# The last loads, the last sums and the last store of a decode kernel: w4 in other pieces, the result on 8 neighbouring partitions, wq in one load

## The chip, the cores and the metric

One core of a Trainium2 chip. The metric is the device time of one execution in microseconds; the tables give medians of several executions. A profile is one execution on the same core; its span is about 1.7 us shorter than the time of that execution (211.0 us of span belong to 212.7 us of time). PE is TensorE, PEld its weight loads, DVE VectorE, ACT ScalarE, POOL GpSimd and SP the engine that issues most loads. A quadrant, in this document, is a group of 32 neighbouring partitions (32i to 32i+31) of a PSUM tile. The granted clock (PEclk) is the share of full speed at which PE was let run, as the profile recorded it.

## The reference, cut to what matters

One decode step for 4 sequences, in bfloat16: an attention over the last 2048 positions of a KV cache and an MLP block, both on the same normalised input, summed.

```python
x = A_x; xn = _layernorm(x)                      # x: 4 x 1 x 576
return x + _A_ref(xn, k_cache, v_cache, wq, wo) + _B_ref(xn, w1, w2, w3, w4)
# _A_ref: q = xn @ wq (576 -> 32 heads x 128); 16 KV heads, 2048 positions; softmax; o @ wo (4096 -> 576)
# _B_ref: with one position the shifted mixer adds nothing, so it is
#         xn + gelu(layernorm(xn) @ w3) @ w4     (576 -> 4608 -> 576)
```

The result has 4 rows of 576 numbers. The kernel treats each as two halves of 288, because its accumulator is a PSUM tile of 288 columns: 8 half rows in all.

## The kernel before: the parts in question

All loads go through one queue on SP, in a fixed order: wq, K and V head by head, wo, w3, and w4 last. w4 (36 blocks of 128 rows, "rows 0 to 35" below) arrives in five pieces, so that PE can begin on the first while the rest is on its way. Half row i of sequence b is summed in partition 32i + 8b of one PSUM tile: the weights of each matmul are 32 columns wide, of which only every eighth is not zero.

```python
for e in range(2):                                # wq: 512 main rows, two loads of 16 KB rows
    lo, hi = e * 2 * NQ, (e + 1) * 2 * NQ
    nc.sync.dma_start(out=wq_sb[:, lo:hi], in_=wq_main[:, lo:hi])
...
W4_PIECES = [0, 10, NFH, NFH + 10, NFH + 14, NF]  # 0, 10, 18, 28, 32, 36
...
def acc_matmuls(lhsT, rhs):                       # QD = 32, CW = 288
    for i in range(2):
        nc.tensor.matmul(out=acc[i * QD:(i + 1) * QD, :], lhsT=lhsT, rhs=rhs[:, i * CW:(i + 1) * CW],
                         start=False, stop=False, skip_group_check=True)
... # the end; hl is the last head
o_turn(hl - 1); o_sum(hl - 1)
mlp_out(*pieces[0])                               # two matmuls for each w4 row in the piece
o_turn(hl); o_sum(hl); o_spread(hl); o_pick(hl)   # the last head's chain: PE, DVE, PE, DVE
mlp_out(*pieces[1])
o_proj(hl)                                        # 16 matmuls with wo
for lo, hi in pieces[2:]:
    mlp_out(lo, hi)
fin = const.tile([2 * QD, CW], out.dtype)
nc.vector.tensor_copy(out=fin[:], in_=acc[0:2 * QD, :])
nc.sync.dma_start(out=o2.rearrange("b (i n) -> i b n", i=2), in_=fin[0:2 * QD:RS, :])   # RS = 8
```

PE runs its instructions in this order: in the trace of this kernel the matmuls of w4 rows 0 to 9 start at 198.94 us and the transposes of the last head's chain at 200.27. If `mlp_out(*pieces[0])` has to wait for its piece, the last head's chain waits behind it.

Of the kernel before, what the change touches and what calls it, by code (L numbers as in the profile page):

```python
# [8 lines left out]
ACT = mybir.ActivationFunctionType  # L9
ALU = mybir.AluOpType  # L10
AX = mybir.AxisListType
BF16 = mybir.dt.bfloat16
F32 = mybir.dt.float32
# [9 lines left out]
def kernel(  # L23
# [14 lines left out]
    nc = tc.nc  # L38
    P = 128
    B, Sq, D = A_x.shape  # L40
# [6 lines left out]
    KJ = 4  # L47
    NQ = Hq * Dh
    NF = F // P
    NFH = NF // 2  # L50
# [3 lines left out]
    QD = 32  # L54
# [3 lines left out]
    CW = D // 2  # L58
# [8 lines left out]
    o2 = out.flatten_outer_dims()  # L67
# [14 lines left out]
    const = ctx.enter_context(tc.tile_pool(name="const", bufs=1))  # L82
# [8 lines left out]
    wo_tiles = {}  # L91
    kv_tiles = {}
    WOH = 8
    WOR = WOH
    WOD = P // WOH
    WOQ = WOH // rep
# [12 lines left out]
    def part(n, parts=P):  # L109
        lo = cut["at"]  # L110
        cut["at"] = lo + n
        assert cut["at"] <= WOR * D
        return first[0:parts, lo:lo + n]
# [2 lines left out]
    nc.scalar.dma_start(out=x_bf[:], in_=x2)  # L116
    wq_sb = wp.tile([P, KJ * NQ + NQ // 2], BF16, tag="w", name="wq_sb")
    wq_main = A_wq[0:KJ * P, :].rearrange("(p j) n -> p (j n)", j=KJ)
    for e in range(2):
        lo, hi = e * 2 * NQ, (e + 1) * 2 * NQ  # L120
        nc.sync.dma_start(out=wq_sb[:, lo:hi], in_=wq_main[:, lo:hi])
    nc.sync.dma_start(out=wq_sb[:, KJ * NQ:], in_=A_wq[KJ * P:D, :].rearrange("r (e f) -> (r e) f", e=2))

    def load_wo(p):
# [9 lines left out]
        nc.sync.dma_start(out=t[:, KJ * F:], in_=B_w3[KJ * P:D, :].rearrange("r (e f) -> (r e) f", e=2))  # L134
        w_tiles["w3"] = t

    W4_PIECES = [0, 10, NFH, NFH + 10, NFH + 14, NF]

    def load_w4():
        t = wp.tile([P, NF, D], BF16, tag="w", name="w4_sb")  # L140
        for lo, hi in zip(W4_PIECES, W4_PIECES[1:]):
            e = lo // NFH
# [8 lines left out]
    ident_f = ident_w[:, 0:P]  # L151
# [7 lines left out]
    def cleared(shape, name):  # L159
        t = const.tile(shape, BF16, name=name)  # L160
        flat = t[:] if len(shape) == 2 else t[:].rearrange("p a b -> p (a b)")
        flat = flat.bitcast(F32)
        nc.scalar.activation(out=flat, in_=zero[:].bitcast(F32).to_broadcast(list(flat.shape)), func=ACT.Copy)
        return t
# [2 lines left out]
    ln2T = cleared([P, KJ + 2, QD], "ln2T")  # L167
    ZP = (NSL - 1) * NJ
    qz = cleared([P, ZP + Hkv * 4 * P], "qz")
    gT = cleared([P, NF, QD], "gT")  # L170
    op = cleared([P, WOR, QD], "op")

    RS = QD // B
    acc = ps_acc.tile([P, CW], F32)
    nc.vector.memset(acc[:], 0.0)


    def layernorm(dst_f, dst_bf, src):
        st = small.tile([B, 2, nc.vector.BN_STATS_DIM], F32, tag="ln_st")
        nc.vector.bn_stats(out=st[:, 0, :], in_=src[:, 0:D // 2])  # L180
        nc.vector.bn_stats(out=st[:, 1, :], in_=src[:, D // 2:D])
        mv = small.tile([B, nc.vector.BN_AGGR_DIM], F32, tag="ln_mv")
        nc.vector.bn_aggr(out=mv[:], in_=st[:].rearrange("p a s -> p (a s)"))
        rstd = small.tile([B, 1], F32, tag="ln_rstd")
        nc.vector.tensor_scalar_add(out=rstd[:], in0=mv[:, 1:2], scalar1=eps)
        nc.gpsimd.tensor_tensor(out=rstd[:], in0=rstd[:], in1=neg_half[:], op=ALU.pow)
        nc.vector.tensor_scalar(out=dst_bf[:], in0=src[:], scalar1=mv[:, 0:1], scalar2=rstd[:, 0:1],
                                op0=ALU.subtract, op1=ALU.mult)
        if dst_f is not None:
            nc.vector.tensor_scalar(out=dst_f[:], in0=src[:], scalar1=mv[:, 0:1], scalar2=rstd[:, 0:1],  # L190
                                    op0=ALU.subtract, op1=ALU.mult)
# [28 lines left out]
    for kb in range(NQD):  # L220
        nc.vector.tensor_copy(out=sel[:, :, :, kb, :],
                              in_=ident_bf[:].rearrange("p (ib i e) -> p ib e i", ib=2, e=2))
# [19 lines left out]
    with nc.allow_low_precision("zeros and ones"):  # L242
# [7 lines left out]
                          in_=sel_j[:].unsqueeze(1).to_broadcast([P, NG, NJ]))  # L250
# [5 lines left out]
    own = const.tile([P, WOH], F32)  # L256
    nc.vector.reduce_sum(out=own[:], in_=ident_f[:].rearrange("p (h d) -> p h d", h=WOH), axis=AX.X)

    idz = const.tile([B, QD], F32)
    nc.gpsimd.memset(idz[:], 0.0)  # L260
    nc.gpsimd.tensor_copy(out=idz[:, 0:QD:RS], in_=ident_f[0:B, 0:B])
    xsum = xn_f
    nc.vector.tensor_tensor(out=xsum[:], in0=xn_f[:], in1=x_bf[:], op=ALU.add)
    for i in range(2):
        nc.tensor.matmul(out=acc[i * QD:(i + 1) * QD, :], lhsT=idz[:], rhs=xsum[:, i * CW:(i + 1) * CW],
                         start=False, stop=False, skip_group_check=True)
    ln2_bf = part(D, B)
    layernorm(None, ln2_bf, xn_bf)
    transposed(ln2_bf, ln2T)
# [24 lines left out]
    for r in range(2):  # L294
        nc.vector.tensor_copy(out=q_bf[:, r],
                              in_=qT_ps[:, r].rearrange("p u (g x) -> p g u x", g=NQD)[:, :, :, 0:B])
    qs_ps = ps_m.tile([P, Hkv, 4, rep, B], F32, tag="m", name="qs_ps")
    for ie in range(4):
        ib, e = divmod(ie, 2)
        nc.tensor.matmul(out=qs_ps[:, :, ie], lhsT=sel[:, ib, e].rearrange("p k i -> p (k i)"),  # L300
                         rhs=q_bf.rearrange("p r g u b -> p (r g u b)"), start=True, stop=True)
# [6 lines left out]
        else:  # L308
            nc.vector.tensor_copy(out=dst, in_=src)  # L309


    def acc_matmuls(lhsT, rhs):
        for i in range(2):
            nc.tensor.matmul(out=acc[i * QD:(i + 1) * QD, :], lhsT=lhsT, rhs=rhs[:, i * CW:(i + 1) * CW],  # L314
                             start=False, stop=False, skip_group_check=True)

    S_ps = {}
    E = {}
# [84 lines left out]
    def o_sum(h):  # L403
        oT = st.pop(("oT", h))
        v = oT[:].rearrange("p s (g x) -> p (s g) x", g=NQD)[:, :, 0:NJ].rearrange("p g (b r) -> p b r g", r=rep)
        k = h % WOQ
        if k == 0:
            st["on"] = small.tile([P, WOH, B], BF16, tag="on", name="on")
        with nc.allow_low_precision("summed in float32"):
            nc.vector.reduce_sum(out=st["on"][:, k * rep:(k + 1) * rep, :].rearrange("p r b -> p b r"),  # L410
                                 in_=v, axis=AX.X)
# [12 lines left out]
    def o_pick(h):  # L424
        if h % WOQ < WOQ - 1:
            return
        R = st.pop("R")
        mk = small.tile([P, WOR, WOH, B], BF16, tag="mk")
        nc.vector.tensor_tensor(out=mk[:], in0=R[:],
                                in1=own[:].unsqueeze(1).unsqueeze(3).to_broadcast([P, WOR, WOH, B]), op=ALU.mult)  # L430
        with nc.allow_low_precision("one term is not zero"):
            nc.vector.reduce_sum(out=op[:, :, 0:QD:RS], in_=mk[:].rearrange("p i h b -> p i b h"), axis=AX.X)

    def o_proj(h):
        if h % WOQ < WOQ - 1:
            return
        for i in range(WOR):
            acc_matmuls(op[:, i, :], wo_tiles[h // WOQ][:, i, :])

    G_CHUNKS = [(e, 4 * g, 4) for e in range(2) for g in range(NQD)] + [(e, 16, 2) for e in range(2)]  # L440
    xs = const.tile([P, NF, B], F32, name="g_x")
# [31 lines left out]
    def mlp_act():  # L473
        u = const.tile([P, NF, B], F32, name="g_u")
        nc.vector.tensor_tensor(out=u[:], in0=xs[:], in1=xs[:], op=ALU.mult)
        nc.vector.tensor_scalar(out=u[:], in0=u[:], scalar1=GELU_A, scalar2=1.0, op0=ALU.mult, op1=ALU.add)
        nc.vector.tensor_tensor(out=u[:], in0=u[:], in1=xs[:], op=ALU.mult)
        nc.scalar.activation(out=u[:], in_=u[:], func=ACT.Tanh, scale=GELU_C)
        nc.vector.tensor_scalar(out=u[:], in0=u[:], scalar1=0.5, scalar2=0.5, op0=ALU.mult, op1=ALU.add)
        nc.vector.tensor_tensor(out=gT[:, :, 0:QD:RS], in0=u[:], in1=xs[:], op=ALU.mult)  # L480

    def mlp_out(lo, hi):
        w4 = w_tiles["w4"]
        for i in range(lo, hi):
            acc_matmuls(gT[:, i, :], w4[:, i, :])


    order = [("K", 0), ("K", 1), ("K", 2)]
# [24 lines left out]
    for t in range(Hkv):  # L513
        hm, hv, hf, hp = t - 1, t - 2, t - 3, t - 4
        for s in range(NSL):
            if s == NSL - 1 and hm >= 0:
                sm_turn(hm)
            n = t * NSL + s + 1
# [26 lines left out]
            if s == 1:  # L545
                if hm >= 0:
                    sm_neg(hm)
                if hf >= 0:
                    o_turn(hf)
                if hp >= 0:  # L550
                    o_proj(hp)
            elif s == 3 and hf >= 0:
                o_spread(hf)
            if t == G_AT:
                if s < 3:
                    mlp_g(s)
                if s > 0:
                    mlp_turn(s - 1)
                if s == NSL - 1:
                    mlp_act()  # L560
# [27 lines left out]
    o_sum(hl - 1)  # L588
    pieces = list(zip(W4_PIECES, W4_PIECES[1:]))
    mlp_out(*pieces[0])  # L590
    o_turn(hl)
    o_sum(hl)
    o_spread(hl)
    o_pick(hl)
    mlp_out(*pieces[1])
    o_proj(hl)
    for lo, hi in pieces[2:]:
        mlp_out(lo, hi)

    fin = const.tile([2 * QD, CW], out.dtype)  # L600
    nc.vector.tensor_copy(out=fin[:], in_=acc[0:2 * QD, :])
    nc.sync.dma_start(out=o2.rearrange("b (i n) -> i b n", i=2), in_=fin[0:2 * QD:RS, :])


# [28 lines left out]
```

## Time and profile before

| | before |
|---|---|
| time, median of 6 (range) | 212.70 us (212.56 to 212.80) |
| bytes loaded | 87.17 MB |
| last w4 piece landed | 206.99 us |
| store issued | 208.21 us |
| end of the span | 210.97 us |

The kernel is bound by its load stream. The list of DMA queues of the kernel before (queue, packets, MB, share of 16 engines' span) says so:

```profile
q1 hardware_dynamic: 6778, 87.17, 97.2%
```

The table of busy time by stretches, again of the kernel before (the last columns are the granted TensorE clock, the share of the DMA engines and GB/s), shows that the stream never pauses between 2.7 and 206.7 us:

```profile
core 0: us, PE busy (x) PEld busy (x) DVE busy (x) ACT busy (x) POOL busy (x), PEclk, DMA share, GB/s
2.70:206.70 204.00, 149.75 (x947) 61.84 (x948) 119.99 (x213) 32.53 (x62) 1.34 (x4) 0.86 1.00 427
206.70:211.00 4.30, 0.67 (x8) 0.34 (x7) 0.45 (x1) 0.00 (x0) 0.00 (x0) 0.86 0.01 3
```

The chain of work that ended last, kernel before, in order of time (start, length, what):

```profile
180.05 26.94 DMA w_sb<-in_B_w_dram
...
207.03 0.68 PE acc L314 x8
...
207.73 0.45 DVE fin L601
```

So after the last byte come eight matmuls, a cast and the store: 4.0 us. With the DMA engines busy throughout (share 1.00) and at the 427 GB/s measured here, only this end, and what piles up in front of it, can be shortened without loading less. The timeline of PE near the end, kernel before (start, length, engine, line, operation, count; in brackets idle time just before and what ended it):

```profile
198.94 1.40 PE L314 MATMUL acc<-w_sb,gT 128*32 128x288 bf16 x20
200.27 0.66 PE L400 MATMUL oT<-ident_w,O_sb 128*128 128x128 f32 x4
201.31 0.35 PE L419 MATMUL R<-on,sel_wo 128*128 128x32 bf16 x8 [0.38 <-DVE on L410]
201.59 1.16 PE L314 MATMUL acc<-w_sb,gT 128*32 128x288 bf16 x16
202.64 1.16 PE L314 MATMUL acc<-wo_sb,op 128*32 128x288 bf16 x16
```

Here PE starts on w4 rows 0 to 9 at 198.94, interleaves the last head's chain with w4 work, and is done with all that has landed before the next piece comes. Twenty matmuls take 1.33 us until the next instruction starts, 66 ns each. The two halves of a pair go to two quadrants and run side by side: in the trace they start within 0.02 us of each other.

### The profile page before, as it was taken

What the parts mean: (1) busy time and instruction counts of PE and PEld (TensorE: products, weight loads), DVE (VectorE), ACT (ScalarE), POOL (GpSimd) and SP (SyncE); (2) the same over time, 40 slices, a digit from 0 to 9 for tenths busy, and PEclk for the clock granted to TensorE, in tenths of its full rate; (3) what the DMA queues carried; (4) which work ended last, traced back from release to release, by engine and by line L of the source; (5) the groups of instructions that cost most, each with busy time, mean ns of one, the idle gap of its engine ahead of it and who ended that gap; (6) DMA issues with size and microseconds to landing.
All of it is one profiled execution on the core that took longest, in us unless ns stands there. A gap on an engine that the chain in (4) does not pass through costs nothing.

```text
span 211.0 us, 2402 instructions
## 1 busy us (share of the span) xinstructions
PE 150.4 (71%) x955; PEld 62.2 (29%) x955; DVE 121.3 (57%) x216; ACT 33.9 (16%) x63; POOL 2.8 (1%) x15
## 2 busy tenths in 40 slices
PE   0386695869395009669999499968693967898982
PEld 0122232224132003214454144334240322433561
DVE  4832989485731082825725968985867284763220
ACT  7703101021102000202121121120211020202300
POOL 4010000000000000000000000000000000000000
PEclk9999579799859655957999669999998596969998
DMA  7999999999999999999999999999999999999990
GB/s 246 435 413 441 422 441 410 443 435 413 450 419 426 438 419 429 434 444 432 416 438 435 416 427 437 435 432 424 436 426 426 420 444 435 422 429 429 425 382 30
DMA packets 6797, 87.32 MB, mean 414 GB/s; under 512 B 758, under 2 KB 770, under 8 KB 1282
## 3 DMA queue, kind: packets, MB, share of 16 engines
q1 hardware_dynamic: 6778, 87.17, 97.2%
q8 instruction: 7, 0.11, 0.2%
q14 instruction: 4, 0.03, 0.0%
q10 hardware_dynamic: 8, 0.00, 0.0%
HBM read 87.17 MB, written 0.00 MB: 413 GB/s over the span
## 4 chain that ended last, share of the span: by engine, by line
DMA 67%; PE 18%; DVE 7%; issue 4%; ACT 1%; SPq 1%; POOL 0%; POOLq 0%; DVEq 0%
DMA w_sb<-in_B_w_dram 29%; DMA vn<-in_A_v_cache_dram 26%; DMA kn<-in_A_k_cache_dram 12%; PE S L335 9%; DVE kt L215 3%; PE g_ps L453 2%; PE q_ps L277 2%; PE O L387 2%; PE oT L400 1%; PE acc L314 1%; DMA first<-in_A_x_dram 1%; DVE qz L309 1%; PE gT_ps L465 1%; DVE mx L341 1%; PE S L357 1%
## 5 line engine op out<-in xcount | busy, mean ns | idle before, releaser
L335 PE MATMUL S<-kt,qz 128*128 128x512 bf16 x256 | 82.0, 452 | 3.1 <-DVE kt L215 3.1
L215 DVE STREAM_TRANSPOSE kt<-kn 128x1024 int32<-128x1024 int32 x64 | 76.8, 1221 | 10.3 <-DMA kn<-in_A_k_cache_dram 9.4
L387 PE MATMUL O<-vn,PT 128*32 128x512 bf16 x256 | 27.8, 434 | 38.5 <-DMA vn<-in_A_v_cache_dram 36.9
L335 PEld LDWEIGHTS <-qz 128*128 128x128 bf16 x256 | 22.2, 106 | 43.2 <-issue 28.5
L363 ACT ACTIVATE E<-S 128x512 bf16<-128x512 f32 x16 | 9.5, 597 | 123.4 <-PE S L357 123.4
L387 PEld LDWEIGHTS <-PT 128*32 128x32 bf16 x256 | 7.3, 95 | 47.2 <-DVE kt L215 23.8
L369 DVE STREAM_TRANSPOSE PT<-E 128x512 bf16<-128x512 bf16 x16 | 11.4, 711 | 14.3 <-ACT E L363 14.3
L353 DVE TENSOR_REDUCE nm<-mg 8x1 bf16<-8x16 f32 x16 | 2.5, 154 | 20.3 <-PE mg L348 20.2
L394 ACT ACTIVATE O_sb<-O,rd 128x512 f32<-128x512 f32 x16 | 11.0, 687 | 16.5 <-issue 11.0
L410 DVE TENSOR_REDUCE on<-oT 128x8 bf16<-128x128 f32 x16 | 4.6, 286 | 15.7 <-PE oT L400 15.7
L400 PE MATMUL oT<-ident_w,O_sb 128*128 128x128 f32 x64 | 11.8, 315 | 0.0
L341 DVE TENSOR_REDUCE mx<-S 128x1 f32<-128x512 f32 x16 | 10.5, 658 | 1.3 <-PE S L335 1.3
L400 PEld LDWEIGHTS oT<-ident_w,O_sb 128*128 128x128 f32 x64 | 9.6, 167 | 5.4 <-issue 3.9
L357 PE MATMUL S<-nm,j_row 8*128 8x512 bf16 x16 | 6.9, 431 | 0.0
L373 PEld LDWEIGHTS dn<-rs,same_j 128*128 128x128 f32 x32 | 5.8, 188 | 2.9 <-ACT E L363 0.7
L326 PE MATMUL S<-negbig,ohT 4*128 4x512 bf16 x16 | 6.2, 385 | 0.0
L314 PE MATMUL acc<-w_sb,gT 128*32 128x288 bf16 x72 | 5.3, 287 | 1.2 <-DMA w_sb<-in_B_w_dram 1.2
L348 PE MATMUL mg<-dm,sel_jb 128*8 128x16 bf16 x16 | 2.8, 175 | 3.7 <-DVE dm L343 3.7
L348 PEld LDWEIGHTS <-sel_jb 128*8 128x8 bf16 x16 | 1.3, 83 | 12.6 <-issue 6.7
L453 PE MATMUL g_ps<-w_sb,ln2T 128*32 128x512 bf16 (+1 forms) x50 | 4.9, 443 | 0.0
L314 PE MATMUL acc<-wo_sb,op 128*32 128x288 bf16 x64 | 4.6, 287 | 0.0
L373 PE MATMUL dn<-rs,same_j 128*128 128x1 f32 x32 | 4.6, 212 | 0.0
(89 smaller groups left out, 72.8 us busy)
## 6 DMA issues: line engine op xcount, KB each, us to landing
kn<-in_A_k_cache_dram SPq DMA_DIRECT2D x16, 2048.0 KB, 22.3
vn<-in_A_v_cache_dram SPq DMA_DIRECT2D x16, 2048.0 KB, 23.9
wo_sb<-in_A_wo_dram SPq DMA_DIRECT2D x4, 1152.0 KB, 25.8
w_sb<-in_B_w_dram SPq DMA_DIRECT2D x2, 2304.0 KB, 31.4
wq_sb<-in_A_wq_dram SPq DMA_DIRECT2D x2, 2048.0 KB, 9.6
w_sb<-in_B_w_dram SPq DMA_DIRECT2D x2, 1440.0 KB, 29.2
w_sb<-in_B_w_dram SPq DMA_DIRECT2D x3, 576.0 KB, 30.5
w_sb<-in_B_w_dram SPq DMA_DIRECT2D x1, 1152.0 KB, 28.7
```

Source lines behind the costliest of these rows:

```text
L215: nc.vector.transpose(out=kt[:], in_=src)
L314: nc.tensor.matmul(out=acc[i * QD:(i + 1) * QD, :], lhsT=lhsT, rhs=rhs[:, i * CW:(i + 1) * CW], start=False, stop=False, skip_group_check= ...
L335: nc.tensor.matmul(out=S_ps[h][:], lhsT=qz[:, z0:z0 + P], rhs=kt[:, ib, :, e:2 * QD:2].rearrange("p c k -> p (c k)"), start=False, stop=Fa ...
L341: nc.vector.reduce_max(out=mx[:], in_=S_ps[h][:], axis=AX.X)
L357: nc.tensor.matmul(out=S_ps[h][:], lhsT=j_row[:], rhs=st.pop(("nm", h))[:, 0:1].to_broadcast([NJ, NW]), start=False, stop=False, skip_grou ...
L363: nc.scalar.activation(out=E[h][:].rearrange("p c k -> p (c k)"), in_=S_ps.pop(h)[:], func=ACT.Exp, scale=scale, accum_out=rs[:])
L369: nc.vector.transpose(out=PT[h][:], in_=E.pop(h)[:])
L373: nc.tensor.matmul(out=dn[:], lhsT=same_j[:], rhs=st.pop(("rs", h))[:], start=True, stop=True)
L387: nc.tensor.matmul(out=O_ps[h][g * QD:(g + 1) * QD], lhsT=PT[h][:, c, :], rhs=vn[:, :, c, :], start=(s == 0), stop=False, skip_group_check ...
L394: nc.scalar.activation(out=O_sb[h][:], in_=O_ps.pop(h)[:], func=ACT.Copy, scale=st.pop(("rd", h))[:, 0:1])
L400: nc.tensor.transpose(out=oT[:, s, :], in_=o[:, s, :], identity=ident_w[:, s * NJ:s * NJ + P])
L453: nc.tensor.matmul(out=g_ps[g * QD:(g + 1) * QD], lhsT=ln2T[:, k, :], rhs=rhs, start=(j == 0), stop=False, skip_group_check=True)
```

## The change

Three things are meant to shorten the two ends of the kernel. The result's 8 half rows come out on neighbouring partitions (2b + i) of one quadrant, so that one plain two-dimensional store writes them. w4's first two pieces become one and the last is cut in two. wq's 512 main rows come in one load. To keep matmuls in pairs, even and odd terms go to two accumulators, on quadrants 0 and 1, except for the last four w4 rows; ACT copies the odd accumulator out and DVE adds it at the end.

```diff
-    for e in range(2):
-        lo, hi = e * 2 * NQ, (e + 1) * 2 * NQ
-        nc.sync.dma_start(out=wq_sb[:, lo:hi], in_=wq_main[:, lo:hi])
+    nc.sync.dma_start(out=wq_sb[:, 0:KJ * NQ], in_=wq_main)
...
-    W4_PIECES = [0, 10, NFH, NFH + 10, NFH + 14, NF]
+    W4_PIECES = [0, NFH, NFH + 10, NFH + 14, NF - 2, NF]
...
+    def acc_matmuls(terms, nq=2):
+        for i in range(2):
+            for n, (lhsT, rhs) in enumerate(terms):
+                q = n % nq
+                nc.tensor.matmul(out=acc[q * QD:q * QD + OR, :], lhsT=lhsT[:, 1 - i:1 - i + OR],
+                                 rhs=rhs[:, i * CW:(i + 1) * CW], start=False, stop=False, skip_group_check=True)
...
-        for i in range(lo, hi):
-            acc_matmuls(gT[:, i, :], w4[:, i, :])
+        for i in range(lo, hi, 2):
+            acc_matmuls([(gT[:, i + u, :], w4[:, i + u, :]) for u in range(2)], 2 if hi <= NF - 4 else 1)
...
-    for lo, hi in pieces[2:]:
+    mlp_out(*pieces[2])
+    odd = const.tile([OR, CW], F32)
+    nc.scalar.activation(out=odd[:], in_=acc[QD:QD + OR, :], func=ACT.Copy)
+    for lo, hi in pieces[3:]:
         mlp_out(lo, hi)
-    fin = const.tile([2 * QD, CW], out.dtype)
-    nc.vector.tensor_copy(out=fin[:], in_=acc[0:2 * QD, :])
-    nc.sync.dma_start(out=o2.rearrange("b (i n) -> i b n", i=2), in_=fin[0:2 * QD:RS, :])
+    fin = const.tile([OR, CW], out.dtype)                  # OR = 8
+    nc.vector.tensor_tensor(out=fin[:], in0=acc[0:OR, :], in1=odd[:], op=ALU.add)
+    nc.sync.dma_start(out=o2.rearrange("b (i n) -> (b i) n", i=2), in_=fin[:])
```

Cut: the tiles `gT`, `op` and `idz`, 10 columns wide instead of 32, whose columns 1, 3, 5 and 7 carry the four sequences, and the residual's matmul.

More of the change, by code (lines that the diff above doesn't have):

```diff
@@ L169 @@
     qz = cleared([P, ZP + Hkv * 4 * P], "qz")
-    gT = cleared([P, NF, QD], "gT")
-    op = cleared([P, WOR, QD], "op")
-    RS = QD // B
+    OR = 2 * B
+    OW = OR + 2
+    gT = cleared([P, NF, OW], "gT")
+    op = cleared([P, WOR, OW], "op")
     acc = ps_acc.tile([P, CW], F32)
     nc.vector.memset(acc[:], 0.0)
+    def acc_matmuls(terms, nq=2):
[4 more added lines that the diff above has]
+                                 rhs=rhs[:, i * CW:(i + 1) * CW], start=False, stop=False, skip_group_check=True)
     def layernorm(dst_f, dst_bf, src):
@@ L257 @@
     nc.vector.reduce_sum(out=own[:], in_=ident_f[:].rearrange("p (h d) -> p h d", h=WOH), axis=AX.X)
-    idz = const.tile([B, QD], F32)
+    idz = const.tile([B, OW], F32)
     nc.gpsimd.memset(idz[:], 0.0)
-    nc.gpsimd.tensor_copy(out=idz[:, 0:QD:RS], in_=ident_f[0:B, 0:B])
+    nc.gpsimd.tensor_copy(out=idz[:, 1:OR + 1:2], in_=ident_f[0:B, 0:B])
     xsum = xn_f
     nc.vector.tensor_tensor(out=xsum[:], in0=xn_f[:], in1=x_bf[:], op=ALU.add)
-    for i in range(2):
-        nc.tensor.matmul(out=acc[i * QD:(i + 1) * QD, :], lhsT=idz[:], rhs=xsum[:, i * CW:(i + 1) * CW],
-                         start=False, stop=False, skip_group_check=True)
+    acc_matmuls([(idz[:], xsum)])
     ln2_bf = part(D, B)
@@ L309 @@
             nc.vector.tensor_copy(out=dst, in_=src)
-    def acc_matmuls(lhsT, rhs):
-        for i in range(2):
-            nc.tensor.matmul(out=acc[i * QD:(i + 1) * QD, :], lhsT=lhsT, rhs=rhs[:, i * CW:(i + 1) * CW],
-                             start=False, stop=False, skip_group_check=True)
     S_ps = {}
@@ L431, in o_pick @@
         with nc.allow_low_precision("one term is not zero"):
-            nc.vector.reduce_sum(out=op[:, :, 0:QD:RS], in_=mk[:].rearrange("p i h b -> p i b h"), axis=AX.X)
+            nc.vector.reduce_sum(out=op[:, :, 1:OR + 1:2], in_=mk[:].rearrange("p i h b -> p i b h"), axis=AX.X)
     def o_proj(h):
@@ L436, in o_proj @@
             return
-        for i in range(WOR):
-            acc_matmuls(op[:, i, :], wo_tiles[h // WOQ][:, i, :])
+        for i in range(0, WOR, 2):
+            acc_matmuls([(op[:, i + u, :], wo_tiles[h // WOQ][:, i + u, :]) for u in range(2)])
     G_CHUNKS = [(e, 4 * g, 4) for e in range(2) for g in range(NQD)] + [(e, 16, 2) for e in range(2)]
@@ L479, in mlp_act @@
         nc.vector.tensor_scalar(out=u[:], in0=u[:], scalar1=0.5, scalar2=0.5, op0=ALU.mult, op1=ALU.add)
-        nc.vector.tensor_tensor(out=gT[:, :, 0:QD:RS], in0=u[:], in1=xs[:], op=ALU.mult)
+        nc.vector.tensor_tensor(out=gT[:, :, 1:OR + 1:2], in0=u[:], in1=xs[:], op=ALU.mult)
     def mlp_out(lo, hi):
         w4 = w_tiles["w4"]
-        for i in range(lo, hi):
-            acc_matmuls(gT[:, i, :], w4[:, i, :])
+        for i in range(lo, hi, 2):
+            acc_matmuls([(gT[:, i + u, :], w4[:, i + u, :]) for u in range(2)], 2 if hi <= NF - 4 else 1)
     order = [("K", 0), ("K", 1), ("K", 2)]
```

## The prediction

> **What bounds it now.** The load stream. The list of DMA queues shows the load queue busy for 97.2% of the 211.0 us span and 87.17 MB moved. The table by stretches gives 427 GB/s and a DMA share of 1.00 from 2.7 to 206.7 us[...]. The chain of waits ends: DMA of w4 to 206.99, eight w4 matmuls (0.68), DVE cast (0.45), store issued at 208.21, end 210.97. What follows the last byte is 4.0 us; only that, and what piles up before it, can move.
>
> **What moves.**
> 1. wq in one 4 MB load: same bytes, same queue. The two halves and the rest landed at 8.11, 12.98 and 14.22 us; the q matmuls start at 12.90 because PE does the second layernorm's transposes first (12.3 to 12.9). The whole load should land at about 12.98. Saved: one 0.4 us issue under a queue that never runs dry. Expected 0, at most 0.1 us.
> 2. w4 pieces. Landings before: rows 0-9 at 198.09, 10-17 at 200.81, 18-27 at 204.23, 28-31 at 205.60, 32-35 at 206.99. After, rows 0-17 land together near 200.81, the two last halves near 206.3 and 207.0. So the first w4 matmuls, which began at 198.94, must wait until 200.85, and there are 36 of them instead of 20. In the timeline 20 take 1.33 us to the next instruction (66 ns each), so 36 take 2.4. The last head's chain (turn, sum, spread, pick), which filled 200.27 to 202.64 beside w4 work, begins only at about 203.25. From the old distances: spread at 204.3, w4 rows 18-27 from 204.55 to 205.9, the output projection's 16 matmuls to 206.95, rows 28-31 to 207.6. PE, which before was idle waiting for DMA at the end (0.47 and 0.72 us), is now behind: rows 32-35 have landed before it gets there.
> 3. Two accumulators on quadrants 0 and 1. The last four rows use one quadrant only, so their eight matmuls cannot run in pairs: about 0.13 us each instead of 0.07 (estimate from the 66 ns of pairs).
> 4. ACT copy of the odd accumulator: by the 64x256 and 128x512 activations (378 and 598 ns) about 0.41 us. In the order of instructions, the matmuls of rows 32-33 wait for this copy, so it is on the chain: 207.65 to 208.1. Then eight serial matmuls, to about 209.2.
> 5. DVE add instead of cast: about 0.45 us, as the 256-column product's 0.43. Store issued near 209.65, 1.45 us later than before.
> 6. Store on 8 neighbouring rows. The trace of before shows 8 packets of 576 B and two semaphore writes[...]. The packets occupied only 209.49 to 209.64, so 0.1 to 0.2 us is saved; 1.28 us to the first packet and 1.3 after the last remain.
>
> Sum: +1.45 - 0.15 = +1.3 us. Elsewhere (matmuls with 8 columns, smaller cleared tiles) nothing is on the load stream's path.
>
> **Prediction:** 214.0 us, 213.1 to 214.8 with 8 in 10. Faster by over 2%: 0.01; within 2%: 0.97; slower: 0.02.
>
> **Right if** the load stream still ends at 207.0; PE stands idle up to 200.8 and then not until the ACT copy; PE waits about 0.4 us for that copy; the last matmuls stand 0.13 us apart; store issue to end falls from 2.76 to about 2.6.
>
> **Wrong if** matmul pairs run faster with 8 columns, so PE catches up; [...]or the 32 KB rows change the stream's rate: 1% is 2 us.

Cuts in the recorded text are marked: a ceiling for the load rate and a rule for the number of DMA engines, which no trace of this case shows, and the clause of "Wrong if" that named these engines. The sum came to +1.3 us: +1.45 for the later issue of the store, -0.15 for the store itself. The 0.1 to 0.2 us of point 6 stand as the author's estimate, whose only measured basis is the 0.15 us that the store's packets took.

## The result

| | before | changed |
|---|---|---|
| time, median of 6 | 212.70 us | 215.07 us |
| range | 212.56 to 212.80 | 213.53 to 216.11 |
| ratio (95% interval) | | 1.0104 (1.0070 to 1.0138) |

A ratio is the mean time of one kernel's fast runs over that of the other's in the same rounds, so it is not quite the ratio of the medians quoted. The changed kernel is slower, and its time now wanders over 2.6 us where the one before kept within 0.25 us. The profiled execution is the slowest, 216.11 us.

The stream itself is as before. Its queue in the changed kernel (same columns), and the stretches:

```profile
q1 hardware_dynamic: 6640, 87.17, 95.6%
```

```profile
core 0: us, PE busy (x) PEld busy (x) DVE busy (x) ACT busy (x) POOL busy (x), PEclk, DMA share, GB/s
2.70:206.70 204.00, 143.79 (x881) 59.54 (x896) 118.83 (x212) 32.11 (x62) 1.32 (x4) 0.85 1.00 425
206.70:214.30 7.60, 4.29 (x60) 2.84 (x59) 1.41 (x4) 0.40 (x1) 0.00 (x0) 0.93 0.01 2
```

The share of 95.6% is lower only because the span is longer. What follows the stream has grown from 4.3 to 7.6 us, and PE now has 4.29 us of work in it instead of 0.67. The end of the chain of work that ended last, changed kernel:

```profile
171.59 29.33 DMA w_sb<-in_B_w_dram
...
200.96 4.48 PE acc L181 x36
...
207.22 2.81 PE acc L181 x44
...
210.05 0.41 ACT odd L598
...
210.50 1.15 PE acc L181 x8
```

The chain no longer waits for the last byte. It leaves the load stream at 200.9 us, at the landing of w4 rows 0 to 17, and from there on PE is the limit. The timeline of the changed kernel shows the same with the waits in brackets:

```profile
200.96 4.48 PE L181 MATMUL acc<-w_sb,gT 128*8 128x288 bf16 x36 [3.42 <-DMA w_sb<-in_B_w_dram]
...
205.37 1.11 PE L399 MATMUL oT<-ident_w,O_sb 128*128 128x128 f32 x4
...
207.15 1.39 PE L181 MATMUL acc<-w_sb,gT 128*8 128x288 bf16 x20
```

The 36 matmuls take 4.41 us until the next instruction, 122 ns each, and the transposes after them 1.11 us instead of 0.66. The 20 matmuls of the same kind at 207.15 take 1.39 us, as before. So these instructions are not slow by nature; they were slow for a while. The table in half microseconds, changed kernel, says for how long (column PEclk):

```profile
199.00:199.50 0.50, 0.00 (x0) 0.00 (x0) 0.00 (x0) 0.00 (x0) 0.00 (x0) 1.00 1.12 479
199.50:200.00 0.50, 0.00 (x0) 0.00 (x0) 0.00 (x0) 0.00 (x0) 0.00 (x0) 0.65 1.05 434
200.00:200.50 0.50, 0.00 (x0) 0.00 (x0) 0.00 (x0) 0.00 (x0) 0.00 (x0) 0.50 0.99 392
...
206.00:206.50 0.50, 0.48 (x3) 0.22 (x2) 0.00 (x0) 0.00 (x0) 0.00 (x0) 0.52 0.44 171
206.50:207.00 0.50, 0.14 (x6) 0.13 (x6) 0.29 (x1) 0.00 (x0) 0.00 (x0) 1.00 0.11 41
```

The clock falls to half within PE's wait of 3.42 us, at about 199.65 (0.65 in that slice means that the first 0.15 us still ran at 1.00), and comes back at about 206.5, 6.8 us later. In the clock's records of this profile and of the kernel before only 1.00 and 0.50 occur; other values, like the 0.65 here, are slices that a switch cuts. The fall came 2.1 us after PE had stopped at 197.54. What sets its moment and its length the trace does not show. In the kernel before, PE's longest wait for a w4 piece was 0.72 us.

### The profile page after: what moved, and what is told of

Read it like the earlier page. It is cut to its first block, busy times and chain, and to the rows that moved or that the text cites. A ratio compares the mean times of both kernels' runs of the same rounds, so it can differ in the third digit from the quotient of the medians.

```text
span 214.3 us, 2389 instructions
## 1 busy us (share of the span) xinstructions
PE 148.1 (69%) x941; PEld 62.4 (29%) x955; DVE 120.7 (56%) x216; ACT 33.9 (16%) x64; POOL 2.7 (1%) x15
## 3 DMA queue, kind: packets, MB, share of 16 engines
q1 hardware_dynamic: 6640, 87.17, 95.6%
## 4 chain that ended last, share of the span: by engine, by line
DMA 66%; PE 21%; DVE 5%; issue 4%; SPq 1%; ACT 1%; POOL 0%; POOLq 0%; DVEq 0%
DMA vn<-in_A_v_cache_dram 36%; DMA w_sb<-in_B_w_dram 30%; PE S L334 7%; PE acc L181 4%; DVE kt L221 2%; PE O L386 2%; PE g_ps L452 2%; PE q_ps L281 2%; PE oT L399 1%; DMA first<-in_A_x_dram 1%; DVE qz L313 1%; PE gT_ps L464 1%; SPq L102 1%; PE S L356 0%; PE qT_ps L296 0%
## 5 line engine op out<-in xcount | busy, mean ns | idle before, releaser
L334 PE MATMUL S<-kt,qz 128*128 128x512 bf16 x242 | 76.9, 441 | 4.9 <-DVE kt L221 3.1
L386 PE MATMUL O<-vn,PT 128*32 128x512 bf16 x256 | 27.2, 425 | 40.7 <-DMA vn<-in_A_v_cache_dram 40.5
L181 PE MATMUL acc<-w_sb,gT 128*8 128x288 bf16 x72 | 7.7, 364 | 3.9 <-DMA w_sb<-in_B_w_dram 3.4
L181 PEld LDWEIGHTS <-gT 128*8 128x8 bf16 x72 | 4.2, 105 | 6.6 <-issue 4.3
L181 PE MATMUL acc<-wo_sb,op 128*8 128x288 bf16 x64 | 4.6, 286 | 0.0
```

Of the source, the lines that this page charges most:

```text
L181: nc.tensor.matmul(out=acc[q * QD:q * QD + OR, :], lhsT=lhsT[:, 1 - i:1 - i + OR], rhs=rhs[:, i * CW:(i + 1) * CW], start=False, stop=Fals ...
L334: nc.tensor.matmul(out=S_ps[h][:], lhsT=qz[:, z0:z0 + P], rhs=kt[:, ib, :, e:2 * QD:2].rearrange("p c k -> p (c k)"), start=False, stop=Fa ...
L386: nc.tensor.matmul(out=O_ps[h][g * QD:(g + 1) * QD], lhsT=PT[h][:, c, :], rhs=vn[:, :, c, :], start=(s == 0), stop=False, skip_group_check ...
```

## The experiments

The theory: merging w4's first pieces makes PE wait up to 3.4 us; in that wait its clock falls to half; the work queued behind runs at half speed, and since PE is then late for everything, the delay reaches the end. The rivals: the 8-column matmuls on alternating quadrants, the two accumulators or the copy cost the time by themselves; or the single wq load does. The experiments were run on four more occasions, each beside the kernel before on the same chip (its medians there: 212.70 to 212.73 us). The versions that take parts of the change alone or leave them out come after those that test the clock.

### Keep PE busy in the wait, first try

```diff
+    fill = ps_s.tile([P, NW], F32, tag="S", name="fill")
+    for _ in range(14):                        # weights: 4 rows x 128; moving: 4 rows x 512
+        nc.tensor.matmul(out=fill[:]..., lhsT=ohT[:], rhs=negbig[:].unsqueeze(1).to_broadcast([B, SC, QD]), ...)
     mlp_out(*pieces[0])
```

> The changed kernel, with 14 matmuls of 512 columns into an unused PSUM tile placed where PE waits for w4 rows 0-17 (about 3 us of work in a 3.4 us wait). Theory (the wait itself only costs what was predicted; the rest is the PE clock, which drops to half in the wait and stays there for the 36 matmuls): the granted clock stays at 1.0 from 197 to 208 us, the 36 matmuls take about 2.4 us instead of 4.4, the head's chain after them loses its 0.45 us too, and every run lies near 213.6 us, within 0.3 of each other instead of over 2.5 us. Rival (the 8-column matmuls on alternating quadrants are slower by themselves): the 36 still take about 4.4 us, times stay at 213.5 to 216 us with the same spread.

Measured: 215.65 us median, 214.78 to 216.34; ratio 1.0135. By its own words this would be the rival's result, but the profile shows that the experiment did not do what it was meant to do. Stretches of this run:

```profile
197.00:200.00 3.00, 3.00 (x18) 1.48 (x17) 0.29 (x1) 0.69 (x1) 0.00 (x0) 1.00 1.00 426
200.00:203.00 3.00, 3.00 (x20) 1.17 (x20) 0.00 (x0) 0.00 (x0) 0.00 (x0) 0.51 0.95 399
```

PE counts as busy all the time from 197 to 203 us, and the clock falls at 200 all the same. Matmuls that use 4 of the array's 128 rows did not hold it (their data, one-hot weights and two constants, also differ from real data; which of the two mattered was not tested). The run rules nothing out, because the clock did fall; it shows that a busy PE in the profile is not enough.

### Keep PE busy in the wait, with the whole array

```diff
+    vf = kv_tiles["V", hl][:].rearrange("p c d -> p (c d)")
+    for n in range(14):                        # weights: 128 x 128; moving: 128 x 512, real data
+        nc.tensor.matmul(out=fill[:], lhsT=wo_tiles[hl // WOQ][:, 0, 0:P], rhs=vf[:, n * NW:(n + 1) * NW], ...)
     mlp_out(*pieces[0])
```

> As the first filler run, but each filler matmul now uses all 128 rows and 128 columns of the array with real data (128x128 weights, 128x512 moving); the first one used 4 rows and did not hold the clock although PE counted as busy. Theory ([...]the clock is the whole excess over the prediction): clock 1.0 from 180 to about 209 us, the 36 matmuls in about 2.4 us, all runs 213.3 to 213.9 us, spread under 0.4. Rival 1 (a drop at about 200 us comes whatever PE does, or the 36 alternating 8-column matmuls are slow by themselves): they stay at 4.4 us and the time at 214.8 to 216.3. Rival 2[...]: a clock below 1.0 inside the filler.

Measured: 213.44 us median, single runs 213.32, 213.33, 213.56 and 214.44; ratio 1.0045. The timeline of this run (it is the one of 214.44 us):

```profile
198.75 3.19 PE L592 MATMUL fill<-vn,wo_sb 128*128 128x512 bf16 x14
...
201.87 2.37 PE L181 MATMUL acc<-w_sb,gT 128*8 128x288 bf16 x36
```

Its clock stood at 1.00 in every stretch from 191 to 209 us, and the same 36 matmuls, unchanged, take 2.37 us. That refutes the rival that they are slow by themselves. The 214.44 us of this execution are 0.9 above the others; here PE reached the filler at 198.75, 1.2 us later than it reached the wait in the changed kernel's profile, so the filler still ran when the piece had landed at 200.78 (PE was free at 201.87): an added cost of the experiment. The spread of 0.4 that was expected was therefore missed by this one run, and so was the clock of 1.0 from 180 us on (it was 0.50 from 185.0 to 188.4). This profile alone does not show that idle PE time caused the drop: arriving at 198.75, PE would have waited only about 2 us without a filler, and the execution below that arrives so late keeps its clock anyway. The next run settles it.

### Half the filler

The same with 7 matmuls instead of 14.

> As the run with 14 full-array filler matmuls, but with 7, so that PE works for 1.6 us and then stands idle for about 1.8 us. It asks how long a wait the clock survives. Theory[...]: no drop in most executions, 36 matmuls in about 2.4 us, 213.3 to 213.7 us. If any wait of 1.8 us is enough: times of 214.8 to 216.2, as in the changed kernel. Between: both kinds of run[...].

Measured: 213.44 us median, 213.31 to 213.55 in all four runs; ratio 1.0033. In the timeline of this run:

```profile
197.47 1.46 PE L592 MATMUL fill<-vn,wo_sb 128*128 128x512 bf16 x6
...
200.85 2.37 PE L181 MATMUL acc<-w_sb,gT 128*8 128x288 bf16 x36 [1.92 <-DMA w_sb<-in_B_w_dram]
```

The stretches of this run, for the clock (one of the seven filler matmuls has no record in the trace, hence x6 above):

```profile
197.15:198.90 1.75, 1.70 (x9) 0.73 (x9) 0.29 (x1) 0.47 (x1) 0.00 (x0) 1.00 0.92 396
198.90:200.85 1.95, 0.03 (x2) 0.04 (x2) 0.00 (x0) 0.00 (x0) 0.00 (x0) 1.00 0.97 401
```

A wait of 1.92 us did not cost the clock in this profile, and the times of the other three runs show no loss either; one of 3.42 us did in the profiles that had it (the changed kernel and "The pieces alone"). This is the cleanest test: PE comes to the wait as early as in the slow execution (its last transposes start at 196.76, there at 196.88), the filler delays nothing, the clock stays, and the wander is gone. Of the eight executions with a full-array filler, none shows the loss of the drop in its time (the 214.44 us above have the other reason), against 7 of 12 without one (next section).

### The changed kernel again

> The changed kernel itself once more, on the same chip as the half filler, for the spread of its times: 213.5 to 216.2 us in steps (no drop 213.5[...]), against 212.6 to 212.9 for the kernel before.

Measured: 214.12 us median of 6, 213.33 to 216.05; ratio 1.0079 (1.0042 to 1.0117). With the first six that makes 5 runs of 12 between 213.33 and 213.60 and 7 between 214.71 and 216.11. Two of the twelve have a profile; that the others fall into the two kinds for the same reason is inferred from their times. This time the profile shows a run of the first kind (213.41 us):

```profile
200.84 2.37 PE L181 MATMUL acc<-w_sb,gT 128*8 128x288 bf16 x36 [1.86 <-DMA w_sb<-in_B_w_dram]
...
207.36 0.40 ACT L598 ACTIVATE odd<-acc 8x288 f32<-8x288 f32 x1 [8.19 <-PE acc L181]
207.81 1.14 PE L181 MATMUL acc<-w_sb,gT 128*8 128x288 bf16 x8 [0.49 <-ACT odd L598]
```

It is the same program, with the landing at the same time. Here PE comes to the wait at 198.98 instead of 197.54, waits 1.86 us, and keeps its clock. Why it comes later can be read from the stretch from 185 to 188 us. First the slow execution of the changed kernel, then this one (columns as above; the last but two is PEclk):

```profile
185.00:188.00 3.00, 2.91 (x20) 1.27 (x20) 2.96 (x7) 0.00 (x0) 0.00 (x0) 1.00 1.02 437
```

```profile
185.00:188.00 3.00, 2.99 (x14) 0.75 (x14) 2.45 (x5) 0.00 (x0) 0.00 (x0) 0.56 1.01 431
```

In the fast execution PE had an earlier half-clock stretch there, did 14 matmuls instead of 20, and so was late, which made the critical wait short. The kernel before also had 0.66 in this stretch in its profile; that is where the arrival time came from on which the prediction built. The profiles of the three filler runs and of the next experiment fit the same pattern (1.00 there: arrival at 197.2 to 197.6; 0.50: at 198.75). This link was seen in seven profiles and was not forced by an experiment. Of the eight other profiles, seven fit too (1.00 there, arrival at 197.3 to 197.5); the eighth, of the last six-piece version below, has 1.00 there, but its half-clock stretch lies later, from 196.83 to 200.24, and PE arrives at 199.66.

Half-clock stretches are thus common in this kernel (the mean granted clock of the kernel before is 0.86); the one at 199.65 differs in that everything after it is on the chain. And the length of a wait does not decide alone. The early stretch of the kernel before, from 185.93 on, follows a wait of 1.45 us:

```profile
185.03 0.40 PE L387 MATMUL O<-vn,PT 128*32 128x512 bf16 x4 [1.45 <-DVE rd L378]
```

In the fast execution of the changed kernel it follows a wait of 1.49 us, while 1.31 us at the same place cost the slow one nothing, and 1.86 and 1.92 us near the end cost nothing either. What else decides was not tested.

### The pieces alone

The kernel before with one line changed:

```diff
-    W4_PIECES = [0, 10, NFH, NFH + 10, NFH + 14, NF]
+    W4_PIECES = [0, NFH, NFH + 10, NFH + 14, NF - 2, NF]
```

> The kernel before, with only the changed w4 pieces. Theory: the same wait until about 200.9 us and the same clock drop, so the first 36 matmuls take up to 4.4 us although they still have 32 columns and one accumulator. No copy on the chain and paired matmuls at the end (about 1 us less than the changed kernel), the old store (0.7 us more): 213.2 us in runs whose clock does not drop, up to 215.8 in those where it does, with a spread of over 1 us. Rival (accumulators and copy cost the time, pieces do not): 212.5 to 212.9 us, no spread.

Measured: 214.44 us median, 212.88 to 215.32; ratio 1.0073 (1.0029 to 1.0116). The range lies 0.3 to 0.5 us below the expected one, the spread is as expected. From its timeline:

```profile
200.86 3.93 PE L314 MATMUL acc<-w_sb,gT 128*32 128x288 bf16 x36 [3.42 <-DMA w_sb<-in_B_w_dram]
```

One accumulator, 32-column weights, no copy, and still the wait of 3.42 us and slow matmuls (by the clock's records in the trace, here for 3.4 us rather than 6.8). The pieces alone bring the loss and the wander. This run also cuts the last piece in two; the six-piece runs below do that too, without loss, so it is the merging that costs.

### Everything but the pieces

The changed kernel with the old pieces, and the copy of the odd accumulator after rows 28 to 31.

```diff
-    W4_PIECES = [0, NFH, NFH + 10, NFH + 14, NF - 2, NF]
+    W4_PIECES = [0, 10, NFH, NFH + 10, NFH + 14, NF]
...
-    mlp_out(*pieces[2])
+    for lo, hi in pieces[2:4]: mlp_out(lo, hi)
     odd = ...
-    for lo, hi in pieces[3:]: mlp_out(lo, hi)
+    for lo, hi in pieces[4:]: mlp_out(lo, hi)
```

> The changed kernel with the old w4 pieces (0-9, 10-17, 18-27, 28-31, 32-35), the copy of the odd accumulator after rows 28-31. Theory: no long wait, clock at 1.0 to the end, PE keeps up with the loads, the copy falls into the wait for the last piece. The last eight matmuls run one after another (1.1 us instead of 0.7), the store costs 2.1 us instead of 2.76: 212.4 us (212.2 to 212.6), spread under 0.3. Rival (two accumulators, 8 columns or the single wq load cost about 1 us by themselves): 213.5 us or more.

Measured: 212.65 us, 212.60 to 212.81; ratio 0.9998 (0.9983 to 1.0013). No wander and no loss; in the profile the clock stands at 1.00 from 180 to 209 us. It is 0.05 us above the range expected; the gain of the store is about eaten by the eight last matmuls, one after another (207.05 to 208.2 instead of 207.7).

### Six pieces, and the copy out of the way

The old pieces with the last cut in two ([0, 10, 18, 28, 32, 34, 36]).

> The changed kernel with six w4 pieces: the old ones, the last cut in two (32-33 and 34-35). Theory: as the run with the old pieces, but only four serial matmuls (about 0.65 us) after the last landing: 212.0 us (211.8 to 212.3), spread under 0.3, faster than before by 0.3%. Rival (the changed accumulators and copy cost about 1 us by themselves): 213 us or more.

Measured: 212.45 us, 212.38 to 212.77; ratio 0.9990 (0.9973 to 1.0007). That is 0.45 us more than expected. The timeline of this run shows why:

```profile
206.41 0.40 ACT L599 ACTIVATE odd<-acc 8x288 f32<-8x288 f32 x1 [8.80 <-PE acc L181]
...
206.87 1.14 PE L181 MATMUL acc<-w_sb,gT 128*8 128x288 bf16 x8 [0.49 <-ACT odd L599]
```

Rows 32 and 33 had landed at 206.39, but their matmuls wait for ACT's copy, although it reads other partitions of the same PSUM tile: in this program the order is kept for the whole tile. The next run gives the odd sum a tile of its own for the tail, and lets the three earlier output projections run on one quadrant:

```diff
+    half["odd"] = ps_acc.tile([P, NW], F32, tag="g", name="acc_odd"); nc.vector.memset(half["odd"][:], 0.0)
...
+                dst = half["odd"] if q else acc
-                nc.tensor.matmul(out=acc[q * QD:q * QD + OR, :], ...
+                nc.tensor.matmul(out=dst[q * QD:q * QD + OR, 0:CW], ...
```

> The six-piece version with the odd accumulator in a PSUM tile of its own (used in the tail only; the three earlier output projections run on one quadrant). Theory (the copy on the chain cost the missing time): matmuls of rows 32-33 start at 206.45 instead of 206.87, the last four end at 207.7 instead of 208.0, 212.1 us (212.0 to 212.3). Rival (the serial matmuls are what is slow, or the three earlier projections on one quadrant hold up the stream): 212.4 us or more.

Measured: 212.27 us, four runs 212.21 to 212.30 and one 212.65; ratio 0.9982 (0.9968 to 0.9996). From its timeline:

```profile
206.45 1.35 PE L184 MATMUL acc<-w_sb,gT 128*8 128x288 bf16 x8
...
206.51 0.40 ACT L604 ACTIVATE odd<-acc_odd 8x288 f32<-8x288 f32 x1 [7.04 <-PE acc_odd L184]
```

Copy and matmuls now run side by side, which shows that the wait came from the shared tile. The time falls by 0.18 us, not the 0.3 hoped for; the intervals of the two versions overlap, so how much the copy cost is not settled closer than that. In this profile the clock stood at 0.50 from 196.83 to 200.24, and yet its time (212.30 us) is as short as the others': with the old pieces PE had caught up when rows 32 and 33 landed at 206.41, so this drop cost nothing. This is the fastest version with a right result, 0.2% ahead of the kernel before, and ahead of the changed one by about 1 to 1.3%.

### wq alone

The kernel before with wq's main rows in one load.

> The kernel before, with wq's 512 main rows in one load. Theory: the load queue is full either way, nothing waits for the first half alone: 212.7 us, within 0.15 of before; the q matmuls start at 13.0 to 13.2 us instead of 12.9 and the load stream ends within 0.2 us of 207.0. Rival (32 KB rows change the stream's rate, or the later q start delays the first transposes): over 0.3 us of difference.

Measured: 212.67 us, 212.47 to 212.83; ratio 0.9999 (0.9982 to 1.0015). In its timeline the q matmuls start at 12.90 us, as before and a little earlier than expected. The load makes no difference.

### The store alone

Two runs change only the last line of the kernel before. Both give a wrong result, because the half rows then land in the wrong places; only the time is looked at. The first stores 8 neighbouring partitions, the second the old spread ones, both to the same plain destination:

```diff
-    nc.sync.dma_start(out=o2.rearrange("b (i n) -> i b n", i=2), in_=fin[0:2 * QD:RS, :])
+    nc.sync.dma_start(out=o2.rearrange("b (i n) -> (b i) n", i=2), in_=fin[0:2 * B, :])       # neighbouring
+    nc.sync.dma_start(out=o2.rearrange("b (i n) -> (b i) n", i=2), in_=fin[0:2 * QD:RS, :])   # spread
```

> The kernel before, but with the plain store of 8 neighbouring partitions of the same tile (wrong result on purpose: these partitions do not hold the 8 half rows; only the store's time is looked at). Theory: the store alone gives what the changed kernel's trace shows, 2.1 us from issue to the end instead of 2.76: 212.05 us (211.9 to 212.25). Rival (the gain in the changed kernel comes from its smaller cast, 8 instead of 64 partitions, or from the later moment of the store): 212.5 to 212.8.

> The kernel before, store from the old partitions 0, 8, ... 56 but to the 8 rows in plain order (wrong result on purpose: half rows land in another order). It tells apart which half of the new store is worth its 0.65 us. If the plain two-dimensional destination[...] is: issue to end 2.1 us and 8 semaphore packets, 212.0 us. If neighbouring partitions are: 2.7 us, 212.7 us.

Measured: neighbouring, 212.24 us (212.19 to 212.29), ratio 0.9978; spread, 212.76 us in its one run. The issue of the store in the timelines, first of the kernel before, then neighbouring, then spread:

```profile
208.21 0.68 SPq L602 DMA_DIRECT2D out_dram<-fin  x1
```

```profile
208.22 0.37 SPq L602 DMA_DIRECT2D out_dram<-fin  x1
```

```profile
208.24 0.72 SPq L602 DMA_DIRECT2D out_dram<-fin  x1
```

And the packets of the store in the view of the DMA queues, cut to the store's time, first before and then spread (8 packets of 576 B carry the rows, those under 512 B are the semaphore writes):

```profile
DMA packets 10, 0.00 MB, mean 6 GB/s; under 512 B 2, under 2 KB 10, under 8 KB 10
```

```profile
DMA packets 16, 0.00 MB, mean 5 GB/s; under 512 B 8, under 2 KB 16, under 8 KB 16
```

The trace shows 2 semaphore writes for the store to 2x4 rows and 8 for the plain one to 8 rows; how many DMA engines each used it does not show. But the spread store has 8 as well and gains nothing. The gain comes from the neighbouring partitions: 0.37 us instead of 0.68 to 0.72 for the issue, and 2.23 us from issue to the end instead of 2.76 (before) and 2.75 (spread). For the spread store this rests on the one profile.

### Two plain stores instead of one

First the kernel before with one store for each half, from spread partitions, on SP and ACT:

> The kernel before with two plain stores, one per half, from partitions 0, 8, 16, 24 on SP and 32, 40, 48, 56 on ACT. If spread partitions make a store slow whatever its number of rows, each takes about 0.7 us to issue and the end comes 2.7 us after the cast as before (212.7 us); if the cost goes with the number of rows, about 0.5 us to issue and 212.4 us.

Measured: 213.62 us in its one run. In its timeline the two issues take 0.76 us on SP and 0.70 on ACT, so four spread partitions cost as much as eight; the span ends 3.52 us after the issue, later than expected in either case. Then a candidate that keeps single accumulators and paired matmuls, with weights of 4 columns:

```diff
-    nc.tensor.matmul(out=acc[i * QD:(i + 1) * QD, :], lhsT=lhsT, ...        # gT, op: 32 columns, every 8th in use
+    nc.tensor.matmul(out=acc[i * QD:i * QD + B, :], lhsT=lhsT, ...          # gT, op: 4 columns
...
+    nc.sync.dma_start(out=o2[:, 0:CW], in_=fin[0:B, :])
+    nc.scalar.dma_start(out=o2[:, CW:D], in_=fin[QD:QD + B, :])
```

> A candidate that keeps what helped and drops what hurt: one accumulator on two quadrants as before (half i in partitions 32i to 32i+3, weights of 4 columns, so matmuls stay in pairs and no copy is needed), six w4 pieces, one cast, two plain stores of 4 neighbouring partitions, on SP and on ACT. Theory: last landing 207.05, 4 paired matmuls to 207.5, cast to 207.95, stores 2.1 us: span 210.1, 211.8 us (211.6 to 212.1), spread under 0.3, clock 1.0 to the end; 0.4% faster than before. If two stores cost more than one: 212.2 us or more.

Measured: 212.72 us, 212.66 to 212.76; ratio 0.9999: the rival's case. Everything up to the stores came as expected; from the timeline of this run:

```profile
207.46 0.45 DVE L597 CAST fin<-acc 36x288 bf16<-36x288 f32 x1 [5.84 <-PE acc L310]
207.94 0.35 SPq L598 DMA_DIRECT2D out_dram<-fin  x1
207.94 0.28 ACTq L599 DMA_DIRECT2D out_dram<-fin  x1
```

The stores are issued 0.27 us earlier than before and fast, but the span still ends at 210.91: 2.97 us after the issue, against 2.23 for one store of neighbouring partitions. The store's last packet is through at 208.91 in the trace, so most of the difference, 2.0 us instead of 1.3, comes after the data. What the program's end waits for with two queues was not resolved; two stores in parallel are not a substitute for one.

## Why the prediction was wrong

- **What bounds the kernel, the stream's end, wq (point 1): right.** The last w4 piece landed at 207.19 instead of 206.99, the stream moved 425 GB/s instead of 427, wq alone changed nothing.
- **The w4 pieces (point 2): right in kind, wrong in one term.** PE did wait, until 200.96 (predicted 200.85), did fall behind, and rows 32 to 35 were there before it came to them. The step that failed is "20 take 1.33 us to the next instruction (66 ns each), so 36 take 2.4". It carried a duration measured at full clock over to work that follows a wait which the change itself creates. In the profiled run they took 4.41 us (122 ns each), and the next transposes and the chain behind them 1.50 us instead of 1.04 to the spread. It also took PE's arrival at 198.94 us, which was one outcome of the clock in one execution, for a constant; in the slow profile it came at 197.5, so that PE waited 3.42 us instead of 1.9. That the clock was what made the duration wrong is shown by the half filler: with PE at work in part of the same wait, the clock stayed and the 36 took 2.30 us until the next instruction (64 ns each).
- **These two terms are the whole difference between the slow and the fast profile.** The profiled spans of 214.33 and 211.63 differ by 2.70 us: 0.12 for the landing, 2.11 for the 36 matmuls (4.41 less 2.30) and 0.46 for the chain behind them.
- **Serial matmuls, copy and add (points 3 to 5): right.** In the fast execution the copy starts at 207.36 (predicted 207.65), PE waits 0.49 us for it (about 0.4), the eight matmuls on one quadrant are through 1.14 us later (1.1; in the slow profile they start 0.12 us apart, predicted 0.13), the add takes 0.45, and the store goes out at 209.53 (209.65).
- **The store (point 6): the reason wrong, the gain too small.** It was put at 0.1 to 0.2 us, for a reason that was never shown; it is 0.46 us by the experiment's medians (212.70 to 212.24), and due to neighbouring partitions: the plain destination alone, with 8 semaphore writes instead of 2, had no effect (212.76 us in its one run). This is why the executions that seem to have kept their clock came at 213.3 to 213.6 us, below the predicted 214.0: in the profiled one the store was issued within 0.12 us of the prediction, and ended 2.10 us later instead of 2.6.
- **The range was wrong in kind.** 213.1 to 214.8 allows for small errors around one value. The time has several values, from 213.3 to 216.1, by whether and how long the clock falls. The chance of 0.97 for "within 2%" held.

## What to carry to other kernels

Merging loads was not free here, where PE works on what has landed: in place of two short waits of PE for w4 (0.47 and 0.72 us) came one of 3.42 us, and a duration measured elsewhere in the trace held only as long as PE's clock did (64 to 66 ns a matmul at 1.00, 122 ns at 0.50). Before moving a wait, ask how long PE will stand idle and what lies behind the wait on the chain, and read the granted clock around it in a profile (even waits of about 1.5 us came before a fall of the clock here); when an otherwise steady time starts to wander in steps (here by up to 2.6 us of 213), look there first. For the small store at the very end of this kernel, neighbouring partitions were worth 0.46 us of 2.8, but only if the sums can be brought there without a copy in front of the last matmuls.
